# Mixed order of small expert units, weight splits on another engine, and an earlier pass over activations, in a fused Fourier-filter and mixture-of-experts kernel

## The chip, the cores and the metric

The kernel runs on one core of one Trainium2 chip. The metric is the device time of one execution in microseconds. A core has TensorE (PE; its weight loads are shown apart, as PEld), VectorE (DVE), ScalarE (ACT), GpSimd (POOL) and SyncE (SP), which issues most of the DMAs; GpSimd issues the DMAs that gather and scatter rows by index.

## The reference, cut to what matters

```python
def _attn_ref(x, filt_r, filt_i):            # x: 8 x 2496 x 256
    X = np.fft.rfft(x, axis=1)
    Y = X * (filt_r + 1j * filt_i)[None, :, :]
    return np.fft.irfft(Y, n=x.shape[1], axis=1).astype(np.float32)

def _moe_ref(x, w_gate, w_noise, noise, w1, w2):   # x: 19968 x 256, 8 experts, F = 1024
    noisy = x @ w_gate + np.log1p(np.exp(x @ w_noise)) * noise
    top2 = np.argpartition(-noisy, 2, axis=1)[:, :2]
    ...                                            # softmax over the two: top2_w
    for e in range(E):
        for k in range(2):
            mask = top2[:, k] == e
            h = np.maximum(x[mask] @ w1[e], 0.0)
            out[mask] += top2_w[mask, k, None] * (h @ w2[e])
```

The eight sequences ("batches") are filtered by a Fourier transform along the sequence, and every row of the result goes through two of eight experts.

## The kernel before, in words

Two streams of work share the engines. **The Fourier stream** (fft_stream) transforms one batch after the other with matrix products, writes the filtered rows to a DRAM tensor `y`, computes the gates, and appends each row's number to its expert's list in DRAM (`lst`). **The expert stream** (expert, fed by parts) takes up to 512 rows of one expert's list at a time, a block: GpSimd gathers the rows (gather), SyncE's DMA transposes them (flip), VectorE copies them apart (turn), TensorE multiplies by w1 (tiles `hps`), ScalarE and VectorE take the ReLU and split it in a high and a low half (`hh`, `hl`), TensorE multiplies by w2 (`yps`), ScalarE scales by the gate (`stage<-yps,gt`), and GpSimd adds the rows to `out` with an indirect DMA, the scatter. A scatter waits until the scatters of the unit ahead of it have landed; those of one unit do not wait for each other.

Every product is three products of halves (_mm3: high with high, high with low, low with high). **Until five batches are through (`ready < HALF`), the halves are float32r**: 21 weight loads of blocks, in each of which wsplit makes four high halves of w1 (`w1h`, ScalarE) and four low halves (`w1l`, 128x512), and the same for w2. From then on the halves are float16 with a power-of-two scale per expert and batch, which needs the largest weight and activation. These come from wscales, a generator that the Fourier stream moves on one step in every fourth of its own (write): 64 loads of weight tiles with a sum of squares each on ScalarE, powers (a short chain over VectorE and TensorE) for w1 and for w2, and 12 loads of rows of `y` of the first two batches, each with a maximum on VectorE (`ymax<-wp`); later batches take their maxima when their rows are written. gather for the first float16 block runs all steps that are then left, one behind the other, until `self.scaled` is set. xscale reduces the maxima to a scale.

**At the end** of the kernel the lists' remainders are done in units: 14 of 256 rows and 4 of 128, each of one expert. A unit loads its two float16 weight planes of 1 MB (load_planes) into one of three sets of buffers (`fr`, `fi`, `wb`), whatever its row count. Gathered rows lie in four slots of 128 rows in `stage`, taken in rotation (slot).

The instruction order on each engine is that of a list scheduler at build time, with parts pinned as written (pin); each engine then runs its list in order.

Of the kernel before, what the change touches and what calls it, by code (L numbers as in the profile page):

```python
# [22 lines left out]
NB, S, D = 8, 2496, 256  # L23
# [26 lines left out]
NUNIT = (LEFT + E * (UNIT // 2 - 1)) // UNIT  # L50
USUAL = LEFT // UNIT
ENDS = (UNIT, USUAL, NUNIT), (UNIT // 2, E // 2, E)
SW = 32
YW = D + E
LR = 128
# [73 lines left out]
def f32v(ap):  # L129
    return ap.bitcast(F32)  # L130
# [20 lines left out]
class Moe:  # L151
# [427 lines left out]
    def xscale(self, bt):  # L579

        nc = self.nc
        nc.vector.tensor_reduce(self.xm, self.ymax[:, :2 * bt + 2], axis=AX.XY, op=ALU.max)
        q = yield from self.powers(self.xm, 1, TX)
        t = self.xs[bt + 1] = self.cp.tile([128, 2], F32, name=f"xs{bt}")
        nc.vector.tensor_copy(t, q[:, :, 0])
        yield

    def wscales(self):


        nc, io, v = self.nc, self.io, self.nc.vector
# [11 lines left out]
        Y = [(bt, h, g) for bt in range(FIRSTS) for h in range(2) for g in range(0, NG, 8)]  # L603
# [27 lines left out]
        def pairs(first, then, n):  # L631
            old = []
            for i in range(n + 3):
                if i >= 3:
                    self.pin(then, *old.pop(0), hold=False)
                if i < n:
                    old.append((i, self.pin(first, i, hold=False)))
                yield

        yield from pairs(load, top, 8 * E)  # L640
        for a, t in enumerate((TW1, TW2)):
            q = yield from self.powers(self.wmax[:, a * E:a * E + E], E, t, True)
# [3 lines left out]
            else:  # L646
                v.tensor_mul(self.wtab[:, 2], self.wtab[:, 2], q[:, 1])
            yield
        yield from pairs(load_y, top_y, len(Y))
        self.scaled = True  # L650
        yield
        self.pin(load_all, 0)
# [483 lines left out]
    def gather(self, blk, i):  # L1136

        nc = self.nc
        lt, n, nt, s, tabi, ready = blk
        if i == 0:  # L1140
            self.ra = nc.gpsimd.value_load(tabi[0:1, 1, s:s + 1], min_val=0, max_val=E - 1)
            self.sc = None
            if ready >= HALF:
                while not self.scaled:
                    next(self.preps)
                self.sc = self.P.tile([128, 3, 1], F32, name="sc", bufs=3)
                nc.gpsimd.tensor_copy(self.sc, self.wtab[:, :, bass.ds(self.ra, 1)])
        w = None
        if self.tail(tabi):
            w = self.wodd = (self.wodd + 1) % 3  # L1150
            if nt < BLK // 128:
                w = self.load_planes(tabi, s, w)
        xg = []
        for t in range(nt):
            x = self.slot("xg")
            self.pin(lambda: nc.gpsimd.indirect_dma_start(  # L1156
                out=x.bitcast(I32), out_offset=None, in_=self.y[:BLK + ready * ROWS],
                in_offset=bass.IndirectOffsetOnAxis(ap=lt[:, i, t:t + 1], axis=0)),
                hold=False, only=[nc.gpsimd.engine])
            xg.append(x)  # L1160
        return xg, self.turns["xg"] + 1 - nt, self.ra, self.sc, w
# [138 lines left out]
    def wsplit(self, st, nm, sc):  # L1300
        nc, P = self.nc, self.P
        if len(st.shape) == 4:
            return st
        if nm == "w2":

            hl = P.tile([128, 2, 2, 256], R32, name="w2", bufs=4)
            h, l = hl[:, 0], hl[:, 1]
        else:
            h = P.tile([128, 2, 256], R32, name=nm + "h", bufs=4)
            l = P.tile([128, 2, 256], R32, name=nm + "l", bufs=4)  # L1310
        sv = st.rearrange("p (k f) -> p k f", k=2)
        if sc is not None:
            if nm == "w1":
                return self.pair(h, l, sv, sc[:, 0])
            hl = hl.rearrange("p a b c -> p (a b c)").bitcast(F16)[:, :1024].rearrange("p (a b c) -> p a b c", a=2, b=2)
            h, l = hl[:, 0], hl[:, 1]
            nc.scalar.activation(h, sv, AF.Copy, scale=sc[:, 1])
            nc.vector.scalar_tensor_tensor(l, sv, sc[:, 1], h, op0=ALU.mult, op1=ALU.subtract)
            return hl
        nc.scalar.copy(h, sv)  # L1320
        nc.vector.tensor_sub(l, sv, f32v(h))
        return hl if nm == "w2" else (h, l)

    def fetch(self, may):
# [81 lines left out]
    def run(self):  # L1406
# [15 lines left out]
        def parts():  # L1422
# [5 lines left out]
            for i in range(NB):  # L1428
# [5 lines left out]
                it = (self.read_list(i, s, m * BLK) for s in range(a, b))  # L1434
# [8 lines left out]
            for s in range(SINGLE):  # L1443
                yield from cut(self.read_list(NB, s, BLK), NB)
            self.more = [self.nc.values_load(self.tabs[NB + 1 + i][0:1, 0, n:n + 1], min_val=0, max_val=E * CAPB * BLK // u)  # L1445
                         for i, (u, n, _) in enumerate(ENDS)]
            it = (self.read_list(NB + 1 + i, s, u) for i, (u, n, _) in enumerate(ENDS) for s in range(n))
            soon = [next(it)]
            while soon:
                soon += [b for b in (next(it, None),) if b]  # L1450
# [14 lines left out]
        for _ in self.expert(parts(), may, fill):  # L1465
# [4 lines left out]
            if state["ready"] >= NB - 1:  # L1470
                state["k"] += 1
                if state["k"] % EVERY == 0:
                    next(self.preps, None)
        with self.tc.If(self.more[0] + self.more[1] < sum(E * CAPB * BLK // u for u, _, _ in ENDS)):
            self.sp = self.spw = None
            rest = (((*self.read_list(NB + 1 + i, s, u), NB), 0) for i, (u, a, b) in enumerate(ENDS) for s in range(a, b))
            for _ in self.expert(rest, lambda: True):
# [43 lines left out]
```

## Time and profile before

| | us |
|---|---|
| median of 3 runs | 2200.29 |
| lowest, highest | 2194.58, 2200.72 |
| the profiled execution's own time | 2191.23 |
| its span in the profile | 2189.4 |

The profile is one execution. Its rows are in microseconds from the start of the span. Lines are those of the kernel before (L1321 is the subtraction in wsplit, L1370 the low half of the ReLU, L1396 the gate's scaling, L1397 the scatter, L1156 the gather, L615 the maximum over rows of `y`, L599 the sum of squares).

### The profile page before, as it was taken

How to read it: one execution, taken by the hardware profiler on the slowest of the kernel's cores; microseconds unless marked ns; L12 is line 12 of the kernel's file. 1: busy time of each engine (PE TensorE's matmuls, PEld its weight loads, DVE VectorE, ACT ScalarE, POOL GpSimd, SP SyncE). 2: the span in 40 equal slices, each digit the busy share in tenths (PEclk: the TensorE clock that was granted, in tenths of full speed). 3: DMA queues.
4: the chain of work that ended last, by engine and by line, in shares of the span. 5: the costliest groups of instructions: out<-in, count | busy, mean ns of one | idle time of the engine just before them, and what ended most of it. 6: DMA issues, size and time to landing. Idle time of an engine off the chain costs nothing. (4 is left out here: it accounts for less than half of the span.)

```text
span 2189.4 us, 42880 instructions
## 1 busy us (share of the span) xinstructions
PE 2107.5 (96%) x14517; PEld 1596.5 (73%) x14517; DVE 1473.3 (67%) x3245; ACT 1286.4 (59%) x2505; POOL 1024.6 (47%) x946
## 2 busy tenths in 40 slices
PE   8779999999999999899999999999999999999996
PEld 6437888888888888666666666766666666667886
DVE  4866678767986787778766886579666664333443
ACT  6666774777567746665665556555566564333443
POOL 4133424533443343545544453544566555654653
PEclk9989999999999999999999999999999999999999
DMA  9688987999888866967766666856899999768996
GB/s 241 173 247 203 230 222 171 222 234 228 203 213 230 189 144 152 202 160 174 156 155 151 136 146 149 198 118 131 198 246 238 230 238 211 200 148 221 277 273 170
DMA packets 511675, 428.49 MB, mean 196 GB/s; under 512 B 215680, under 2 KB 397016, under 8 KB 511448
## 3 DMA queue, kind: packets, MB, share of 16 engines
q1 hardware_dynamic: 450135, 341.27, 59.2%
q0 software_dynamic: 61312, 84.40, 22.5%
q8 instruction: 116, 1.90, 0.4%
q14 instruction: 112, 0.91, 0.1%
HBM read 263.92 MB, written 122.03 MB: 176 GB/s over the span
## 5 line engine op out<-in xcount | busy, mean ns | idle before, releaser
L1397 POOL DMA_INDIRECT out<-stage,ids x316 | 527.3, 1669 | 339.8 <-ACT stage L1396 245.9
L1370 DVE SCALAR_TENSOR_TENSOR hl<-hps,hh 128x512 f16<-128x512 f32 (+3 forms) x712 | 432.2, 624 | 339.5 <-ACT hh L1369 279.1
L1156 POOL DMA_INDIRECT stage<-y,ids x316 | 348.4, 1103 | 538.2 <-DMA xt<-stage 425.5
L124 PE MATMUL yps<-w,hh 128*128 128x256 f16 (+1 forms) x2048 | 558.8, 279 | 9.0 <-ACT hh L1369 3.8
L125 PE MATMUL yps<-w,hh 128*128 128x256 f16 (+1 forms) x2048 | 553.2, 277 | 0.0
L126 PE MATMUL yps<-w,hl 128*128 128x256 f16 (+1 forms) x2048 | 543.4, 278 | 6.8 <-DVE hl L1370 6.5
L1369 ACT ACTIVATE hh<-hps 128x512 f16<-128x512 f32 (+3 forms) x712 | 375.6, 550 | 185.7 <-PE hps L126 161.6
L125 PE MATMUL hps<-mxl,w1h 128*128 128x512 f16 (+1 forms) x1024 | 394.3, 386 | 0.7 <-DVE mxl L1244 0.7
L126 PE MATMUL hps<-mxh,w1l 128*128 128x512 f16 (+1 forms) x1024 | 393.0, 385 | 0.0
L124 PE MATMUL hps<-mxh,w1h 128*128 128x512 f16 (+1 forms) x1024 | 385.5, 388 | 2.7 <-DVE hl L1370 1.7
L1396 ACT ACTIVATE stage<-yps,gt 128x256 f32<-128x256 f32 x316 | 143.2, 475 | 342.3 <-PE yps L126 169.8
L124 PEld LDWEIGHTS <-hh 128*128 128x128 f16 x1760 | 172.3, 98 | 51.3 <-ACT hh L1369 4.1
L126 PEld LDWEIGHTS <-hl 128*128 128x128 f16 x1760 | 171.5, 98 | 48.9 <-issue 3.0
L125 PEld LDWEIGHTS <-hh 128*128 128x128 f16 x1760 | 172.2, 98 | 38.1 <-issue 6.0
L126 PEld LDWEIGHTS yps<-w,hl 128*128 128x128 f32 x768 | 145.9, 192 | 15.8 <-DVE hl L1370 8.2
L124 PEld LDWEIGHTS yps<-w,hh 128*128 128x128 f32 x768 | 147.0, 192 | 12.5 <-ACT hh L1369 4.9
L125 PEld LDWEIGHTS yps<-w,hh 128*128 128x128 f32 x768 | 146.6, 192 | 4.4 <-issue 0.6
L542 ACT COPY yt<-q 117x1024 uint16<-117x1024 uint16 x96 | 90.8, 946 | 42.4 <-PE q L536 23.6
L126 PEld LDWEIGHTS <-w1l 128*128 128x128 f16 x640 | 62.6, 98 | 71.8 <-issue 1.1
L1226 DVE COPY stage<-xt 128x1024 uint16<-128x1024 uint16 (+2 forms) x174 | 109.8, 685 | 3.0 <-issue 1.9
L125 PEld LDWEIGHTS <-w1h 128*128 128x128 f16 x640 | 62.6, 98 | 54.0 <-issue 4.0
L124 PEld LDWEIGHTS <-w1h 128*128 128x128 f16 x640 | 62.6, 98 | 53.0 <-issue 6.2
(287 smaller groups left out, 4041.7 us busy)
## 6 DMA issues: line engine op xcount, KB each, us to landing
stage<-w SPq DMA_DIRECT2D x328, 256.0 KB
x<-x SPq DMA_DIRECT2D x88, 256.0 KB
fd<-c SPq DMA_DIRECT2D x77, 240.0 KB
fi<-wpl SPq DMA_DIRECT2D x18, 1024.0 KB
fx<-fd SPq DMA_DIRECT2D x140, 128.0 KB
out<-z SPq DMA_DIRECT2D x24, 702.0 KB
wp<-w SPq DMA_DIRECT2D x64, 256.0 KB
fr<-w SPq DMA_DIRECT2D x16, 1024.0 KB
```

The source lines that it names most:

```text
L124: nc.tensor.matmul(o, lh, rh, start=start, stop=False)
L125: nc.tensor.matmul(o, lh, rl, start=False, stop=False)
L126: nc.tensor.matmul(o, ll, rh, start=False, stop=stop)
L542: e = nc.scalar.copy(yt.bitcast(U16)[:, :k, :256].rearrange("p g (two d) -> p g two d", two=2), p.bitcast(U16)[:RP, :2 * m].rearrange("p ( ...
L1156: self.pin(lambda: nc.gpsimd.indirect_dma_start(out=x.bitcast(I32), out_offset=None, in_=self.y[:BLK + ready * ROWS], in_offset=bass.Indir ...
L1226: nc.vector.tensor_copy(xu.rearrange("p (t two) -> p two t", two=2), ent[3][0][:, 2 * kc:2 * kc + 2, :w])
L1369: hold(lambda: nc.scalar.activation(h, p, AF.Relu))
L1370: v = hold(lambda: nc.vector.scalar_tensor_tensor(l, p, 0.0, hf[0], op0=ALU.max, op1=ALU.subtract))
L1396: nc.scalar.activation(o, p, AF.Copy, scale=gate[:, t])
L1397: a = nc.gpsimd.indirect_dma_start(out=self.io["out"][:BLK + ready * ROWS], out_offset=bass.IndirectOffsetOnAxis(ap=ids[:, t:t + 1], axis= ...
```

## The change

There are four edits. parts takes the small units in an order written in MIXED: after every third unit of 256 rows or so stands one of 128, the last of them at the end. gather skips slots so that a unit's rows begin at a multiple of its own row count. wsplit subtracts on GpSimd in place of VectorE for w1 as long as the halves are float32r. wscales runs its 12 loads and maxima over `y` first, then the 64 sums over the weights; a flag `seen` marks that the maxima are done, and xscale asserts it.

```diff
+MIXED = sorted(((i, s) for i, (_, n, _) in enumerate(ENDS) for s in range(n)), key=lambda u: u[1] * 3 + 4 if u[0] else u[1])
...
     def xscale(self, bt):
 
         nc = self.nc
+        assert self.seen
...
+        yield from pairs(load_y, top_y, len(Y))
+        self.seen = True
         yield from pairs(load, top, 8 * E)
         for a, t in enumerate((TW1, TW2)):
             q = yield from self.powers(self.wmax[:, a * E:a * E + E], E, t, True)
...
-        yield from pairs(load_y, top_y, len(Y))
         self.scaled = True
...
+        while (self.turns.get("xg", -1) + 1) % nt:
+            self.slot("xg")
         xg = []
...
-        nc.vector.tensor_sub(l, sv, f32v(h))
+        (nc.gpsimd if nm == 'w1' else nc.vector).tensor_sub(l, sv, f32v(h))
...
-            it = (self.read_list(NB + 1 + i, s, u) for i, (u, n, _) in enumerate(ENDS) for s in range(n))
+            it = (self.read_list(NB + 1 + i, s, ENDS[i][0]) for i, s in MIXED)
```

Three places show what moves on the engines. Between them, from about the 31st block of the expert stream to the units, the orders are the same on every engine, and they are the same up to the first blocks.

GpSimd, one block of the float32r part, before: `gt` is the gate copy for the next block, `stage<-y` the gathers for the one after, `out<-stage` the scatters of an earlier block.

```order
L1178 COPY gt<-stage 128x4
L1156 DMA stage<-y,ids 128x264 x4
L1106 CAST ids<-lt 128x4
L1397 DMA out<-stage,ids 5660x256 x4
L1178 ISA
```

The same place in the change:

```order
L1183 COPY gt<-stage 128x4
L1326 TENSOR_TENSOR w1l<-stage,w1h 128x512 x3
L1161 DMA stage<-y,ids 128x264 x2
L1326 TENSOR_TENSOR w1l<-stage,w1h 128x512
L1161 DMA stage<-y,ids 128x264 x2
L1109 CAST ids<-lt 128x4
L1402 DMA out<-stage,ids 5660x256 x4
L1183 ISA
```

Three of a block's four subtractions stand between the gate copy and the first gather, the fourth behind two gathers.

VectorE, before, where the float32r part ends (the 23rd and 24th block): `ymax<-wp` are the maxima over rows of `y`, `hl` is the low half that TensorE's second product needs.

```order
L1370 SCALAR_TENSOR_TENSOR hl<-hps,hh 128x512 x2
L547 TENSOR_REDUCE ymax<-yt 117x1
L582 TENSOR_REDUCE xm<-ymax 128x1
L615 TENSOR_REDUCE ymax<-wp 117x1 x2
L1202 SCALAR_TENSOR_TENSOR w1l<-stage,sc,w1h 128x512
L1370 SCALAR_TENSOR_TENSOR hl<-hps,hh 128x512
L398 TENSOR_TENSOR tl<-fx,th 128x512
L615 TENSOR_REDUCE ymax<-wp 117x1
L1370 SCALAR_TENSOR_TENSOR hl<-hps,hh 128x512
```

The same place in the change, with the last two reductions over the weights' sums (`wmax`):

```order
L548 TENSOR_REDUCE ymax<-yt 117x1
L584 TENSOR_REDUCE xm<-ymax 128x1
L603 TENSOR_REDUCE wmax<-wquart 128x1
L399 TENSOR_TENSOR tl<-fx,th 128x512
L562 TENSOR_REDUCE pm<-xm 1x1
```

and the first of the 12 maxima in the change, at the second block of the expert stream:

```order
L1082 TENSOR_TENSOR ro<-ro,rx 56x128
L1249 TENSOR_TENSOR mxl_2204<-xps,mxh_2203 128x512
L617 TENSOR_REDUCE ymax<-wp 117x1
L1375 SCALAR_TENSOR_TENSOR hl<-hps,hh 128x512
L341 TENSOR_TENSOR xl<-x,xh 117x512
```

The 12 maxima left the end of the float32r part and stand within the second to fourth block of the stream. The 64 sums of squares on ScalarE all stood ahead of the 20th block, 13 of them ahead of the fourth; now none stands ahead of the fourth, and the last 11 stand between the 20th and the 23rd.

GpSimd, the end of the program, before: gate copies of one column are those of the 128-row units.

```order
L1397 DMA out<-stage,ids 21104x256 x2
L1178 ISA
L1178 COPY gt<-stage 128x1
L1180 TENSOR_SCALAR gt<-gt,sc,xs_20026 128x1
L1397 DMA out<-stage,ids 21104x256
L1178 ISA
L1178 COPY gt<-stage 128x1
L1180 TENSOR_SCALAR gt<-gt,sc,xs_20026 128x1
L1397 DMA out<-stage,ids 21104x256 x3
```

The same place in the change:

```order
L1402 DMA out<-stage,ids 21104x256 x2
L1183 ISA
L1183 COPY gt<-stage 128x1
L1185 TENSOR_SCALAR gt<-gt,sc,xs_20026 128x1
L1402 DMA out<-stage,ids 21104x256 x5
```

Before, the last four scatters are of four units of one scatter each. In the change the last five are two, two and one: two units of 256 rows and one of 128.

## Rows read from the trace of the kernel before

**Rows 1.** Windows: PE, PEld, DVE, ACT, POOL busy; TensorE clock; DMA share; GB/s.

```profile
200.00:850.00 650.00, 634.38 (x4090) 554.57 (x4089) 504.18 (x1105) 440.67 (x891) 267.41 (x217) 0.99 0.86 205
850.00:900.00 50.00, 42.99 (x279) 36.04 (x278) 36.10 (x63) 27.77 (x54) 24.33 (x23) 0.97 0.95 191
900.00:2000.00 1100.00, 1091.55 (x7596) 742.38 (x7595) 727.62 (x1474) 613.53 (x1121) 575.02 (x531) 1.00 0.78 181
2000.00:2150.00 150.00, 149.95 (x1381) 133.67 (x1380) 65.18 (x170) 65.66 (x171) 86.51 (x107) 1.00 1.05 260
2150.00:2174.00 24.00, 22.79 (x286) 20.27 (x283) 11.26 (x43) 10.86 (x40) 8.67 (x10) 1.00 0.72 211
```

**Rows 2.** Timeline of GpSimd, a scatter at 2122 and the last three.

```profile
2122.46 1.54 POOL L1397 DMA_INDIRECT out<-stage,ids  x1 [0.30 <-issue]
...
2169.94 1.59 POOL L1397 DMA_INDIRECT out<-stage,ids  x1 [6.30 <-ACT hh L1369]
2175.61 1.56 POOL L1397 DMA_INDIRECT out<-stage,ids  x1 [4.08 <-ACTq L1474]
2180.16 1.56 POOL L1397 DMA_INDIRECT out<-stage,ids  x1 [2.99 <-DMA out<-stage,ids]
```

**Rows 3.** Timeline of ScalarE: the gate's scaling ahead of these scatters.

```profile
2121.45 0.47 ACT L1396 ACTIVATE stage<-yps,gt 128x256 f32<-128x256 f32 x1 [1.75 <-PE yps L126]
...
2168.68 0.47 ACT L1396 ACTIVATE stage<-yps,gt 128x256 f32<-128x256 f32 x1 [0.85 <-issue]
...
2174.12 0.47 ACT L1396 ACTIVATE stage<-yps,gt 128x256 f32<-128x256 f32 x1 [0.86 <-PE yps L126]
```

**Rows 4.** The chain that ended last, in order of time: one piece.

```profile
2175.61 3.80 DMA out<-stage,ids
```

**Rows 5.** DMA issues of the page: a weight plane of the units.

```profile
fi<-wpl SPq DMA_DIRECT2D x18, 1024.0 KB
```

**Rows 6.** Window of 50 us in the units, columns as in rows 1.

```profile
2050.00:2100.00 50.00, 50.00 (x459) 44.49 (x458) 22.64 (x59) 22.41 (x58) 31.42 (x40) 1.00 1.07 281
```

**Rows 7.** Waits of TensorE from 869 to 896: us in total, times, longest.

```profile
PE yps L126 <- DVE hl L1370: 4.2, 2, 3.4
PE q L446 <- DVE a L428: 1.3, 1, 1.3
```

**Rows 8.** Groups on VectorE from 869 to 892: busy, mean ns, idle before.

```profile
L615 DVE TENSOR_REDUCE ymax<-wp 117x1 f32<-117x1024 bf16 (+1 forms) x9 | 10.0, 1125 | 4.1 <-DMA wp<-y 3.8 <-issue 0.3
```

**Rows 9.** Window of 5 us behind that wait, columns as in rows 1.

```profile
880.00:885.00 5.00, 3.35 (x15) 3.05 (x16) 4.75 (x7) 2.62 (x5) 3.92 (x4) 0.66 1.28 172
```

**Rows 10.** Single lines: duration ns min/median/max, first and last start.

```profile
L615 DVE TENSOR_REDUCE ymax<-wp x12: 929/1204/1221, 839.2 to 890.0; 117x1 f32<-117x1024 bf16 x8, 117x1 f32<-117x768 bf16 x4
L599 ACT ACTIVATE wp<-wp x64: 621/632/708, 187.4 to 734.8; 128x512 f32<-128x512 f32 x64
```

**Rows 11.** Groups by form: the subtraction on VectorE, a subtraction of that size on GpSimd.

```profile
L1321 DVE TENSOR_TENSOR w1l<-stage,w1h 128x512 fp32r<-128x512 f32 x84 | 57.7, 694 | 9.1 <-ACT w1h L1320 7.0 <-PE q L510 1.4 <-issue 0.6
L433 POOL TENSOR_TENSOR ab<-ab 128x512 f32<-128x512 f32 x10 | 12.7, 1271 | 9.5 <-DVE ab L432 9.5
```

**Rows 12.** Timeline of GpSimd in the float32r part: gate copy, first gather.

```profile
522.45 0.78 POOL L1178 COPY gt<-stage 128x4 f32 x1
530.91 1.02 POOL L1156 DMA_INDIRECT stage<-y,ids  x1 [7.68 <-DMA xt<-stage]
```

**Rows 13.** Timeline of VectorE in the same stretch: low halves of weights and rows.

```profile
533.29 0.69 DVE L1321 TENSOR_TENSOR w1l<-stage,w1h 128x512 fp32r<-128x512 f32 x1
534.49 0.68 DVE L1244 TENSOR_TENSOR mxl<-stage,mxh 128x512 fp32r<-128x512 f32 x1
```

**Rows 14.** Timeline at 70: VectorE beside a GpSimd subtraction, and alone.

```profile
69.73 1.35 DVE L894 TENSOR_TENSOR oh<-gz,m 117x176 f32<-117x176 f32 x1
...
72.98 0.34 DVE L894 TENSOR_TENSOR oh<-gz,m 117x176 f32<-117x176 f32 x1
...
69.62 1.26 POOL L428 TENSOR_TENSOR ab<-ab 128x512 f32<-128x512 f32 x1 [19.33 <-ACT yt L542]
```

## The prediction

> **What bounds the kernel now.** Read first the windows by stage [rows 1]. TensorE is busy for nearly every microsecond: it idles 15.6 us from 200 to 850 (650 less 634.38), 7.0 from 850 to 900, 8.5 from 900 to 2000, nothing from 2000 to 2150, 1.2 from 2150 to 2174, and then 15 us pass to the end of the span without a product. Since the change adds and removes no product, it can win only such idle time, or make more of it. The instruction order differs in two stretches: the first thirty blocks (to about 1000 us) and the units (from about 2000). So three places count: the last 15 us, the 7.0 us around 875, and the float32r part, in which the new work of GpSimd and VectorE must find cover.
>
> **The end: small units among large ones.** The last row of the chain that ended last is a scatter's DMA of 3.80 us, from its start to the landing [rows 4], and behind it the last scatter starts at 2180.16 [rows 2]. Its data was ready long before: ScalarE's last scaling ended at 2174.12 + 0.47 = 2174.59 [rows 3]. Where nothing holds a scatter, it starts soon after its scaling: 2121.45 + 0.47 = 2121.92 on ScalarE [rows 3], 2122.46 on GpSimd [rows 2], 0.54 us. So the last one could start at 2175.13 and starts 5.0 us later. It waits because each 128-row unit is one scatter that must wait for the landing of the one before; the last three start at 2169.94, 2175.61 and 2180.16 [rows 2], each held, while the scalings behind them are 2174.12 - 2168.68 = 5.44 us apart [rows 3]. In the new order a unit of 256 rows stands ahead of the last unit of 128. Its second tile is scaled by about 2169.15, its scatter starts at 2169.7 and lands 3.80 us later at 2173.5, before 2175.13. The wait is gone: -5.0 us. TensorE's 1.2 us of idle time among the four small units [rows 1] should partly go, since a small unit's chain then lies beside a large unit's products: -0.5, between -1.2 and 0.
>
> What this costs is DMA. A unit loads two planes of 1024 KB [rows 5], 2.10 MB, whatever its rows. A unit of 256 rows is 48 products of 256 columns and 48 of 256, 24576 columns, 10.24 us at 2.4 GHz, the level that a granted clock of 1.00 is [rows 1]. At 260 GB/s [rows 1] it moves 2.66 MB, so 0.56 MB beside the planes. Three large units and a small one want 4 x 2.10 + 3.5 x 0.56 = 10.36 MB in 3 x 10.24 + 5.44 = 36.2 us, 286 GB/s. The highest window shows 281 [rows 6], with TensorE at 50.00 of 50; by that the group takes 36.9 us, 0.7 more. If 260 were the ceiling, it would take 39.8, and three groups would lose 11 us, less what the buffers cover: a load is issued two units ahead, at least 10.24 + 5.44 = 15.7 us, and 2.10 MB at 260 GB/s take 8.1, so 7.6 are covered and about 3.5 stay. I take nothing, because the rate that is wanted is nearly one that was seen with no idle time; bound +3.5. Skipped slots cost no work; a gather may come half a unit later, which the two units of lead hide.
> The end: **-5.5 us**, bounds -6.2 and -1.5.
>
> **The float32r part's end: the maxima leave.** From 869 to 896 TensorE waits 4.2 us for VectorE's `hl` and 1.3 for its `a` [rows 7]. VectorE is late there because nine of the twelve maxima over `y` stand in that stretch: 10.0 us of work and 4.1 of waiting, most of it for their loads [rows 8], 14.1 of 23 us. After the longer wait the granted clock is 0.66 for 5 us with 3.35 of work [rows 9], a third of which is lost, about 1 us. Without the maxima: -6.5 us; at worst the wait is passed to something else, 0.
> In their place come the last 11 sums of squares, at 0.632 us [rows 10] 7.0 us on ScalarE, which is busy 27.77 of 50 there [rows 1], and they wait for loads too. If ScalarE's lateness reached TensorE as VectorE's did (5.5 us for 14.1), it would cost 5.5 x 7.0 / 14.1 = 2.7. I take +1.5, about the middle, as ScalarE has more room.
>
> **The float32r part's start: the maxima come.** Twelve maxima of 1.2 us [rows 10] are 14.4 us on VectorE in the first four blocks, with their loads. At the old rate, 5.5 us for nine, they would cost 7.3; but the subtractions of four blocks, 16 x 0.694 = 11.1 us [rows 11], leave VectorE there, and 13 sums leave ScalarE, 8.2 us. I take +2.5, bounds 0 and 7.3.
>
> **The subtraction on GpSimd.** 84 subtractions of 128x512 leave VectorE, 57.7 us, and cost 1.271 us each on GpSimd by the nearest row, 107 us [rows 11]. GpSimd has the time: 267 of 650 us are busy from 200 to 850 [rows 1]. What counts is where it sits in the queue. Behind the gate copy at 522.45 to 523.2 GpSimd waits 7.68 us for a transposition [rows 12]; the three subtractions that stand there in the new order take 3.8. The fourth stands behind two gathers of about a microsecond and starts near 534 or 535, where VectorE did it at 533.29, just before the rows' last low half at 534.49 [rows 13]; it is needed only in the last quarter of the products by w1, some 8 us on. Loads of w2 into the same slots wait for it on SyncE's queue, and transpositions stand behind them: a few tenths of a microsecond late per block. No gain either, since VectorE is not what TensorE waits for in most of this part. I take +1, bounds -2 (VectorE's relief) and +14 (see below).
> VectorE pays in another way. Beside a GpSimd subtraction that started at 69.62 and took 1.26, a small operation of VectorE took 1.35, and the same operation 0.34 when alone [rows 14]: it stood still until GpSimd was done. So the relief of 57.7 us shrinks by up to 84 x 1.01 = 85 us.
> The Trainium skill's page "SBUF — State Buffer", section "Who interferes with whom", speaks against this edit with just that: a VectorE instruction with two SBUF inputs and a GpSimd instruction that reads SBUF share a port, and the later one blocks wholly until the earlier ends. The trace agrees, by 1.01 us at the row named; by the page in full this edit's term would be the port's case among the rivals, by my reading of the rows it is the +1 above.
>
> **Sum.** -5.5 - 6.5 + 1.5 + 2.5 + 1 = -7.0 us. The profiled execution's 2191.23 would become 2184.2. It lies 9 us below the median of the runs, 2200.29, from which the forecast is **2193 us**.
>
> **Rivals.**
> *Only the end pays.* The generator's work is only traded between places: what the maxima cost at 875 they cost again at the start, and the sums the rest. For it: VectorE is as busy over 200 to 850 (504 of 650) as around 875 (36 of 50), and DMA is busy too (0.86) [rows 1]. Against: the subtractions leave. Time 2200.3 - 5.5 = 2195, within 0.3%.
> *The shared port decides.* If every subtraction holds VectorE for 1.01 us, VectorE gains 85 - 57.7 = 27 us of load; if half of that reaches TensorE, +13.5, in place of my +1. Against: the operation that was held reads both inputs from SBUF, while `hl`, which TensorE waits for, reads one from PSUM, and no row shows such a one held. 2193 + 12.5 = 2206; if only a quarter reaches it, 2199.
> *The subtraction is late: slower than before.* GpSimd's queue is in order, and a block's products by w1 cannot go on without `w1l`. If the late transposition or a held scatter keeps GpSimd from the subtractions, each of 21 weight loads stalls TensorE. It decides once 21 stalls eat the other terms and 0.3% more: (8.0 + 6.6) / 21 = 0.7 us each. At 1 us each: 2200.3 - 8 + 21 = 2213. For it: scatters stand ahead of the subtractions. Against: the 7.68 us of idle time [rows 12].
> *Planes come late among the units.* +3.5 and the idle gain lost: 2197.
>
> **Chances.** 0.3% of the time, 6.6 us, is about what a measurement of this kernel can tell from no change, and 2193 lies just beyond it. My forecast or better has 0.50, of which 0.05 would still read as the same; only the end 0.22 (0.02 faster, the rest the same); the port 0.11 (0.08 the same, 0.03 slower); the late subtraction 0.10, slower; the planes 0.07, the same. Faster 0.47, same 0.40, slower 0.13. The likeliest case alone runs from 2187 to 2197. For 8 in 10 I take 2185 to 2207: from every term at its good bound (-6.2 - 6.5 + 0 + 0 - 2, 2186, and a microsecond for the runs) to the port's case.
>
> **What would show it.** In the changed profile the last scatter starts within a microsecond of ScalarE's last scaling, and no two single scatters follow each other. No wait for `hl` over 2 us stands around 875. `w1l` takes about 1.3 us on GpSimd, lies in the gap behind the gate copy, and TensorE waits for GpSimd less than 3 us in all; some of VectorE's two-input operations take a microsecond more. In the units TensorE stays at full busy time. I am wrong if TensorE waits for GpSimd's `w1l` or VectorE's `hl` block after block, if the maxima make waits of several us near 200, or if a unit's first product waits for its plane.

## The result and the profile after

The changed kernel takes 2222.62 us (median of 6 runs, 2219.69 to 2228.79), the kernel before 2195.41 beside it (2190.59 to 2200.72): ratio 1.0127, 95% interval 1.0104 to 1.0149. It is 27 us slower where 2193 us, 0.3% faster, was forecast, and it lies outside the range. Its profiled span is 2220.1 us against 2189.4.

The windows by stage, columns as in [rows 1], the last one shifted to the changed kernel's end:

```profile
200.00:850.00 650.00, 611.97 (x3885) 526.49 (x3884) 503.52 (x987) 423.09 (x858) 349.57 (x286) 0.99 0.85 202
850.00:900.00 50.00, 47.74 (x310) 40.94 (x309) 30.11 (x79) 27.93 (x60) 20.36 (x22) 1.00 0.68 159
900.00:2000.00 1100.00, 1089.44 (x7556) 745.63 (x7556) 729.16 (x1477) 616.54 (x1128) 566.60 (x522) 1.00 0.78 176
2000.00:2150.00 150.00, 147.66 (x1312) 122.81 (x1311) 62.21 (x159) 61.62 (x159) 78.45 (x98) 1.00 0.96 254
2150.00:2210.00 60.00, 58.23 (x566) 50.51 (x565) 25.19 (x72) 26.49 (x73) 30.10 (x33) 1.00 0.84 222
```

Against [rows 1] TensorE idles 38.0 us from 200 to 850 instead of 15.6, and 2.3 us from 2000 to 2150 instead of none; from 850 to 900 it is busy 4.75 us more. VectorE, which was to be relieved by 57.7 us, is as busy as before from 200 to 850: 503.5 against 504.2.

Windows of time hide that the two kernels are at different work at one time. So count the products of the expert blocks (`hps`, `yps`; 11856 in both) and take each one's start, from the two traces:

| start of product | before | after | later by |
|---|---|---|---|
| 1536 | 501.4 | 515.9 | 14.6 |
| 3840 | 978.6 | 1002.9 | 24.3 |
| 8704 | 1782.2 | 1814.5 | 32.3 |
| the last | 2173.8 | 2210.1 | 36.3 |
| end of the span | 2189.4 | 2220.1 | 30.7 |

Of the 36.3 us, 24.3 are lost by product 3840, in the early, float32r stretch. Another 8.0 lie between products 3840 and 8704, where the instruction orders are the same. These can't be put down to the change: products 4224 to 8704 stand in one order in all twenty kernels whose traces are used here, and take 735.1 to 748.2 us in them (739.5 before, 748.2 after; the ten that take 735 are those of the sets of runs below in which the kernel before took 2178 to 2179 us). Among the units 4 us more go, and behind the last product 5.6 us come back, the gain that the end was to bring. That gain can be read on ScalarE and GpSimd. The first fence is ScalarE's last scaling, the second GpSimd's last two scatters (answering to [rows 3] and [rows 2]):

```profile
2210.41 0.47 ACT L1401 ACTIVATE stage<-yps,gt 128x256 f32<-128x256 f32 x1 [0.86 <-PE yps L127]
```

```profile
2206.82 1.56 POOL L1402 DMA_INDIRECT out<-stage,ids  x1 [0.62 <-ACT stage L1401]
2211.70 1.56 POOL L1402 DMA_INDIRECT out<-stage,ids  x1 [3.33 <-DMA out<-stage,ids]
```

2210.88 to 2211.70 is 0.8 us, where it was 5.6.

In the early stretch TensorE waits nowhere for GpSimd's subtraction by name. These are TensorE's largest waits from 200 to 850 (total, times, longest):

```profile
PE yps L127 <- DVE hl L1375: 8.9, 7, 2.5
PE yps L125 <- ACT hh L1374: 6.2, 5, 2.5
PE hps L125 <- DVE hl L1375: 4.3, 7, 1.4
PE yps L125 <- ACT stage L1401: 3.2, 2, 1.7
PE q L447 <- DVE a L429: 2.9, 2, 2.1
```

Many short waits, for VectorE and ScalarE. The subtraction itself, on GpSimd (group by form; answers to [rows 11]), and the waits of SyncE's queue for it from 150 to 980:

```profile
L1326 POOL TENSOR_TENSOR w1l<-stage,w1h 128x512 fp32r<-128x512 f32 x84 | 117.7, 1433 | 99.1 <-ACT w1h L1325 93.0 <-DMA stage<-w 5.4 <-DMA fd<-c 0.3
```

```profile
SPq L1287 <- POOL w1l L1326: 55.0, 39, 6.1
```

The subtraction takes 1.43 us on average, and SyncE's queue stands 55.0 us in all behind it.

### The profile page after: what moved, and what is told of

It reads as the page before. It is cut to its first block, busy times and chain, and to the rows that moved or that the text cites. A ratio compares the mean times of both kernels' runs of the same rounds, so it can differ in the third digit from the quotient of the medians.

```text
span 2220.1 us, 42897 instructions
## 1 busy us (share of the span) xinstructions
PE 2121.4 (96%) x14517; PEld 1595.5 (72%) x14517; DVE 1486.2 (67%) x3161; ACT 1283.1 (58%) x2505; POOL 1116.8 (50%) x1030
## 4 chain that ended last, share of the span: by engine, by line
PE 59%; DVE 3%; issue 1%; DMA 1%; ACT 1%; POOL 0%; POOLq 0%; DVEq 0%; SPq 0%; ACTq 0%
PE yps L127 9%; PE hps L127 9%; PE yps L125 9%; PE hps L125 9%; PE yps L126 9%; PE hps L126 9%; PE q L447 1%; DMA wp<-w 1%; DVE hl L1375 1%; PE q L511 1%; PE u L458 0%; PE q L535 0%; ACT hh L1374 0%; PE q L536 0%; PE q L537 0%
## 5 line engine op out<-in xcount | busy, mean ns | idle before, releaser
L1161 POOL DMA_INDIRECT stage<-y,ids x316 | 340.3, 1077 | 472.6 <-DMA xt<-stage 365.4
L1326 POOL TENSOR_TENSOR w1l<-stage,w1h 128x512 fp32r<-128x512 f32 x84 | 117.7, 1433 | 99.1 <-ACT w1h L1325 93.0
L1231 DVE COPY stage<-xt 128x1024 uint16<-128x1024 uint16 (+2 forms) x174 | 128.1, 788 | 0.0
L126 PEld LDWEIGHTS <-w1h 128*128 128x128 f16 x640 | 62.7, 98 | 58.3 <-issue 9.1
```

What stands on the lines that cost most here:

```text
L126: nc.tensor.matmul(o, lh, rl, start=False, stop=False)
L1161: self.pin(lambda: nc.gpsimd.indirect_dma_start(out=x.bitcast(I32), out_offset=None, in_=self.y[:BLK + ready * ROWS], in_offset=bass.Indir ...
L1231: nc.vector.tensor_copy(xu.rearrange("p (t two) -> p two t", two=2), ent[3][0][:, 2 * kc:2 * kc + 2, :w])
L1326: (nc.gpsimd if nm == 'w1' else nc.vector).tensor_sub(l, sv, f32v(h))
```

## The experiments

Each is timed beside the kernel before on the same chip. From one set of runs to the next that kernel's median lay between 2178.1 and 2195.3 us (on one and the same chip at 2190.9 and 2178.1), so ratios to it are compared, not times.

### Each edit alone

**The changed kernel without the subtraction's edit, the subtraction alone, the maxima alone, the units alone.** The first and second edit one line:

```diff
-        (nc.gpsimd if nm == 'w1' else nc.vector).tensor_sub(l, sv, f32v(h))
+        nc.vector.tensor_sub(l, sv, f32v(h))
```

(the second the other way round, in the kernel before); the third moves `yield from pairs(load_y, top_y, len(Y))` ahead of the weights' `pairs`; the fourth has MIXED and the slots' alignment alone.

> The changed kernel with the first-layer float32r subtraction back on VectorE; the unit order and the maxima stay as changed. Theory (the subtraction costs the time): at equal counts of expert matmuls the changed kernel had lost 24 us by its 3840th, all inside the stretch in which GpSimd subtracts, so this kernel stands about 24 to 30 us under the changed one, 2193 to 2199 us, within 0.3% of the kernel before. Rival (the maxima ahead of the weights' sums, by moving VectorE's work into the first 250 us, cost the time): it stays near 2215 to 2223.

> The kernel before with the one line of the subtraction on GpSimd. Theory: the loss comes with this line alone, 20 to 30 us above the kernel before, 2215 to 2226 us. Rival (the maxima cost it): 2195 within 5 us.

> The kernel before with the y maxima ahead of the weights' sums. Theory (the subtraction costs the time): within 0.3% of the kernel before, and if the prediction's terms hold (6.5 us of waits near 870 leave, 1.5 and 2.5 come back) 2.5 us under it, 2193. Rival (the maxima cost the time): 15 to 27 us above it, 2210 to 2222.

> The kernel before with units of 128 rows among those of 256 and the slots' alignment alone. The prediction has 5.5 us under the kernel before, 2190. The rival from the changed kernel's trace: the end after the last matmul is 5.6 us shorter (10.0 against 15.6 us), but the matmuls' starts in the units stretch lose 4.0 us more in waits for the hand-offs, so that only about 1.5 us are left, 2194.

| kernel | us | ratio | 95% interval |
|---|---|---|---|
| changed, without the subtraction's edit | 2222.55 | 1.0140 | 1.0108 to 1.0172 |
| the subtraction alone | 2231.30 | 1.0187 | 1.0153 to 1.0220 |
| the maxima alone | 2221.04 | 1.0115 | 1.0085 to 1.0146 |
| the units alone | 2198.21 | 1.0019 | 0.9997 to 1.0040 |

The theory that the subtraction alone costs the time fell: without it nothing comes back. But the subtraction alone costs more (36 us) than all edits together (27), and so the costs do not add. Both edits share one thing: the scheduler, which orders by simulated times, makes a new order of all engines from the first blocks to about the 30th whenever one early instruction changes. The maxima's edit changes no instruction's engine, shape or number, only order. So order and engine had to be separated.

The units alone leave the early stretch alone (product 3840 starts 0.5 us later, 8704 at the same time). Their last product starts 10.3 us later and the end of the span comes 5.1 us later, so 5.2 us come back at the end, as forecast, and twice that is lost before. TensorE's waits from 1900 to 2190:

```profile
PE yps L125 <- ACT hh L1372: 4.2, 6, 0.9
PE hps L125 <- ACT mxh L1204: 0.4, 1, 0.4
PE hps L125 <- DMA fi<-wpl: 0.3, 1, 0.3
```

In the kernel before, from 1900 to 2180, the first of these is

```profile
PE yps L124 <- ACT hh L1369: 0.8, 3, 0.3
```

and two windows with the units alone (columns as in [rows 1]):

```profile
2050.00:2065.00 15.00, 13.40 (x138) 10.98 (x136) 5.62 (x18) 5.39 (x16) 10.42 (x13) 1.00 1.04 303
2065.00:2070.00 5.00, 4.53 (x24) 2.88 (x22) 1.17 (x4) 1.96 (x6) 1.79 (x6) 0.66 1.07 242
```

Five of the six waits for ScalarE's relu (`hh`) stand within 4 us of a seam, a change between large and small units; the likely reason, which is not tested, is that a small unit's products are too short to cover it. Behind 1.6 us of idle time the granted clock is 0.66 over 5 us, a mean of the levels of 2.4 and 1.2 GHz. The named waits make 4.9 of the 10.3 us, the lower clock in this window about 1.7 (0.34 of 5 us); the rest has no name in the trace. The planes are nearly innocent: one wait of 0.3 us in all, and none in the window that shows 303 GB/s.

**The four small units together, one large unit last.**

```diff
-MIXED = sorted(..., key=lambda u: u[1] * 3 + 4 if u[0] else u[1])
+MIXED = sorted(..., key=lambda u: USUAL - 1.5 if u[0] else u[1])
```

> The kernel before with the slots' alignment and another order of the units: thirteen of 256 rows, the four of 128, and the last of 256 behind them. Theory (a last unit of 256 rows saves 5.3 us behind the last matmul, 10.1 against 15.3 us, and the units of 128 that stand apart cost 10.4 us in hand-offs, as the waits before their matmuls show): with the four together only two changes of size remain, the hand-offs cost 1 to 3 us and 2 to 4 us stay, 2191 to 2194. Rival (any unit of 256 behind one of 128 waits for its planes): no gain, 2195 to 2199.

2192.58 us, 1.0005 (0.9986 to 1.0024). No gain that can be told, and none lost; a gain of 2 to 4 us is at the edge of this interval, so the two theories are not told apart by the time. The rival's mechanism does not show in the trace: no product among the units waits for a plane by name. The longest wait there, 3.5 us, is for VectorE's `hl` in the last small unit.

### The order held

Order-only dependencies (they wait for nothing but the place in the queue) between each instruction and the one ahead of it in a recorded order hold every engine to that order:

```diff
+def hold_order(tc, bb):
+    here, last = {i.name: i for i in bb.instructions}, {}
+    for n in names:                # the recorded order
+        i = here.get(f"I-{n}")
...
+            tc.add_manual_dep(i, p.name, mybir.DependencyInfo(
+                mybir.DependencyClass.NoSync, mybir.DependencyReason.DATA), reason="order as recorded")
```

**The subtraction on GpSimd in the order of the kernel before**, and **the order that the subtraction's edit makes, with the subtraction on VectorE.**

> The kernel before with the first-layer float32r subtraction on GpSimd, and every engine's order held to that of the kernel before by order-only dependencies, so that the 84 subtractions alone change their engine. Theory (the new order of the whole early stretch costs the 36 us of the same edit, not GpSimd): 2188 to 2202 us, within 0.3% of the kernel before. Rival (GpSimd's slower subtraction, its queue or the shared port costs it): 2215 to 2232.

> The other corner: all engines held to the order that the scheduler made for the subtraction on GpSimd, but the subtractions stay on VectorE, so that no instruction changes its engine against the kernel before. Theory (the order costs it): 2220 to 2235 us, as with the subtraction on GpSimd in that order (2231). Rival (the engine costs it): 2190 to 2202.

| order | subtraction on VectorE | on GpSimd |
|---|---|---|
| of the kernel before | 1 | 2210.44 us, 1.0085 (1.0059 to 1.0110) |
| made for GpSimd | 2212.97 us, 1.0099 (1.0076 to 1.0123) | 1.0187 (above) |

Neither theory is right alone: the engine costs 0.85%, the order 0.99%, and together they make the 1.87%. Some 19 us come from 84 instructions on another engine, and some 22 us from an order in which nothing changes its engine. (In the traces the order on every engine is indeed the recorded one, but for a few neighbours that start together.)

What the engine does can be seen here with nothing else moved. Groups by form from 150 to 1000 on VectorE, before and then with the subtraction on GpSimd:

```profile
L1226 DVE COPY stage<-xt 128x1024 uint16<-128x1024 uint16 x54 | 37.4, 746 | 2.7 <-issue 1.9 <-DMA xt<-stage 0.8
L1244 DVE TENSOR_TENSOR mxl<-stage,mxh 128x512 fp32r<-128x512 f32 x44 | 30.0, 682 | 1.2 <-ACT mxh L1243 0.8 <-issue 0.2
```

```profile
L1226 DVE COPY stage<-xt 128x1024 uint16<-128x1024 uint16 x52 | 47.3, 963 | 1.8 <-issue 1.6 <-DMA xt<-stage 0.2
L1244 DVE TENSOR_TENSOR mxl<-stage,mxh 128x512 fp32r<-128x512 f32 x44 | 43.6, 991 | 2.0 <-ACT mxh L1243 1.7 <-issue 0.2
```

The rows' low halves `mxl`, which stand next to the weights' in every block, rise from 682 to 991 ns, 1821 for the 12 that overlap a subtraction. The extreme, VectorE first, then GpSimd:

```profile
394.88 4.79 DVE L1244 TENSOR_TENSOR mxl<-stage,mxh 128x512 fp32r<-128x512 f32 x1
```

```profile
394.78 4.33 POOL L1321 TENSOR_TENSOR w1l<-stage,w1h 128x512 fp32r<-128x512 f32 x3
```

One VectorE instruction of 0.68 us stands through three subtractions in a row and ends behind the last. Over 150 to 1040, 169 VectorE instructions overlap a subtraction and take 45.4 us more than their own medians in the kernel before; 57.7 us of relief shrink to 12. `hl`, which reads PSUM, is not lengthened: 44 of the 169 are `hl`, at a mean of 683 ns, and its longest of the 216 from 150 to 1000 is 694 ns.

TensorE feels it. Its waits for VectorE from 150 to 980 make 11.0 us in the kernel before and 20.3 us here; those for ScalarE rise from 16.7 to 21.0, those for GpSimd from nothing to 1.5. (Both are sums over the rows of the view of TensorE's waits.) The window, columns as in [rows 1], and two of those rows, before:

```profile
150.00:980.00 830.00, 803.49 (x5153) 679.25 (x5154) 634.31 (x1397) 553.97 (x1099) 333.54 (x281) 0.99 0.85 201
PE yps L126 <- DVE hl L1370: 6.2, 5, 3.4
PE hps L125 <- DVE mxl L1244: 0.7, 2, 0.4
```

and with the subtraction on GpSimd, with two rows that are new:

```profile
150.00:980.00 830.00, 789.33 (x5019) 670.77 (x5020) 616.01 (x1281) 541.44 (x1075) 425.05 (x353) 0.98 0.84 196
PE yps L126 <- DVE hl L1370: 3.6, 2, 2.7
PE hps L125 <- DVE mxl L1244: 3.5, 3, 1.7
PE yps L126 <- DVE w1l L1202: 3.6, 1, 3.6
PE q L534 <- DVE tl L521: 3.3, 1, 3.3
```

The same can be asked of every pair of kernels here that have one order and differ in the subtraction's engine: the order of the kernel before as it is, with late squares and with small loads (both below), the order made for GpSimd, and the changed kernel's order as it is and with late squares. In all six pairs TensorE's waits for VectorE grow with the subtraction on GpSimd, by 5 to 13 us; its waits for ScalarE change by -1.5 to +4.3 us and those for GpSimd by at most 2.9. Each trace is a single execution, but the six agree. And SyncE's queue waits for `w1l`, before and now:

```profile
SPq L1282 <- DVE w1l L1321: 22.9, 17, 7.4
```

```profile
SPq L1282 <- POOL w1l L1321: 53.0, 35, 9.4
```

These waits do not make the queue slower as a whole: all its waits from 150 to 980 are 375.5 us before and 359.3 us here. The queue waits longer for `w1l` and less for other things.

**Lateness without GpSimd**: the subtraction on VectorE, later in VectorE's held order, and **the subtraction on GpSimd in four pieces**, in the held order of the kernel before:

```diff
-        (nc.gpsimd if nm == 'w1' else nc.vector).tensor_sub(l, sv, f32v(h))
+        if nm == 'w1':
+            for k in range(2):
+                for o in (0, 128):
+                    nc.gpsimd.tensor_sub(l[:, k, o:o + 128], sv[:, k, o:o + 128], f32v(h)[:, k, o:o + 128])
+        else:
+            nc.vector.tensor_sub(l, sv, f32v(h))
```

> The order of the kernel before held, the subtraction on GpSimd in four pieces of 128x128 instead of one of 128x512 (in one piece: 1.0085 of the kernel before). Theory (VectorE's instructions beside the subtraction stand until it ends, 45 us in all): they can go in between pieces, the 45 us fall to under 25 and the ratio to 1.002 to 1.006. Rival (the planes' low parts are late by GpSimd's own time): four instructions take longer than one of 1.3 us, and the ratio is 1.0085 to 1.013.

> The order of the kernel before held, the subtraction on VectorE, but 71 of its 84 instructions 1 to 4 VectorE instructions later, so that the planes' low parts come later without GpSimd. On GpSimd their mean time behind the high part rose from 1.73 to 2.64 us and the ratio to 1.0085. Theory (VectorE's instructions that stand beside GpSimd's are what costs, not the lateness): ratio 0.998 to 1.003. Rival (the lateness costs it): 1.005 to 1.010.

In pieces: 2204.50 us, 1.0106 (1.0085 to 1.0128), by the rival. But it does not decide: the time that VectorE loses beside them fell only from 45.4 to 39.3 us, while the four pieces of a plane take 2.2 us (172.6 / 80, the first fence, a group by form) instead of 1.4, and the queue's wait rose to 74.0:

```profile
L1324 POOL TENSOR_TENSOR w1l<-stage,w1h 128x128 fp32r<-128x128 f32 x320 | 172.6, 627 | 60.2 <-ACT w1h L1320 37.2 <-DVE oc L1059 18.9 <-ACT th L520 2.4
```

```profile
SPq L1282 <- POOL w1l L1324: 74.0, 49, 6.1
```

Late on VectorE: 2192.99 us, 1.0063 (1.0041 to 1.0085), the rival's too. The low half's mean distance behind the high half (end to end, over 84) is 1.73 us before, 2.64 on GpSimd and 3.10 here; the queue's wait:

```profile
SPq L1282 <- DVE w1l L1321: 63.5, 31, 11.8
```

So lateness alone costs: 1.37 us for each of 84 instructions is 0.63%, though TensorE's waits for `w1l` stay at 0.2 us in all. The way from there to TensorE is not shown. The load of the next weights into the freed slot waits for the subtraction, and on SyncE's queue everything stands behind that load; but a longer wait of that queue is not by itself a loss. All its waits are 398.6 us here, 375.5 in the kernel before, and 401.5 in the kernel with small loads below, which is the fastest of all.

If the cost is in proportion, GpSimd's 0.91 us make 0.42% of its 0.85% (an estimate from these two runs), and the other half is left for what VectorE stands beside GpSimd. The pieces do not fit that split well: their low halves end 2.11 us later than in the kernel before (3.84 us behind the high half), which by the same proportion is 0.97% of their 1.06%, though VectorE still loses 39.3 us beside them. So lateness is at work for certain, VectorE's standing beside GpSimd probably, and how the 0.85% divides between them stays open. What speaks for VectorE's part is TensorE's waits: late on VectorE, the subtraction raises those for VectorE by 3.2 us and those for ScalarE by 6.0; on GpSimd it is 9.3 and 4.3.

### Where an order loses

**Late squares.** On ScalarE the squares of the weights' sums stand so early that they wait for their 256 KB load, and ScalarE with them. Their group from 150 to 1000, in the kernel before, with the maxima alone, and in the order made for GpSimd with the subtraction on VectorE:

```profile
L599 ACT ACTIVATE wp<-wp 128x512 f32<-128x512 f32 x64 | 40.9, 640 | 53.6 <-DMA wp<-w 45.7 <-issue 7.0 <-DVE wmax L601 0.6
```

```profile
L600 ACT ACTIVATE wp<-wp 128x512 f32<-128x512 f32 x64 | 40.7, 635 | 62.7 <-DMA wp<-w 61.2 <-DVE rx L1080 1.1 <-DVE wmax L602 0.2
```

```profile
L599 ACT ACTIVATE wp<-wp 128x512 f32<-128x512 f32 x64 | 40.6, 635 | 70.5 <-DMA wp<-w 69.2 <-issue 1.2
```

So the squares were moved behind up to 4 of ScalarE's next instructions (where needed VectorE's reductions over the sums move with them), the rest of the order held: in the kernel before, with the maxima alone, with the subtraction on GpSimd, and in the other order. Only the recorded list of the order differs from the kernel that each starts from.

> The kernel before, its order held except that 48 of the 64 squares of the weights' sums on ScalarE stand 4 ScalarE instructions later, and 9 others up to 3 later (7 can't move). In the kernel before 33 squares wait in ScalarE's queue for their 256 KB load, 45.9 us in all, 50.1 to 70 us in the slower orders. Theory (ScalarE's waits for these loads are what an order gains or loses by): those waits fall under 15 us and the time by 5 to 15 us, to 2180 to 2190. Rival (they lie beside other work): 2193 to 2200, no change.

> The kernel with the maxima's edit alone (2221 us), its order held except that 48 of the 64 squares on ScalarE stand 4 of its instructions later. ScalarE waits 61.3 us there for the squares' loads, 45.9 us in the kernel before. Theory (this edit's loss comes through these waits): 2200 to 2212 us. Rival (as in the kernel before, where the same step took 31.7 us of such waits away and the time stood still): 2216 to 2226.

> Subtraction on GpSimd in the order of the kernel before (2210 us), with the squares 4 ScalarE instructions later. Theory (late weight loads hold SP's queue, behind it a square's load comes late, and ScalarE stands 5 to 6 us at 514 and 715 us): 2193 to 2202. Rival (GpSimd's instruction stretches VectorE's beside it, 45 us in all, and that costs the time): 2206 to 2214.

> The order that the scheduler made for the subtraction on GpSimd, the subtraction on VectorE (1.0099 of the kernel before), with the squares on ScalarE up to 4 instructions later. ScalarE waits 69.2 us for the squares' loads in that order. Theory (this order loses by the squares' waits, as the maxima's edit did): 1.002 to 1.006. Rival (it loses in other places): 1.008 to 1.012.

| order | waits for the loads, us | ratio without | with late squares |
|---|---|---|---|
| of the kernel before | 45.7 to 14.2 | 1 | 1.0009 (0.9993 to 1.0026) |
| the maxima alone | 61.2 to 27.0 | 1.0115 | 1.0039 (1.0022 to 1.0056) |
| before, subtraction on GpSimd | 57.6 to 21.3 | 1.0085 | 1.0084 (1.0060 to 1.0109) |
| made for GpSimd, on VectorE | 69.2 to 16.8 | 1.0099 | 1.0051 (1.0031 to 1.0070) |

Two new orders get back two thirds and a half of their loss. The old order, where as much waiting was taken away, gains nothing, and GpSimd's part is not touched. The waits are thus one channel of a new order's loss, and not worth their length: where the order is the old one, TensorE's work covers them.

**Small loads.** In the kernel before, and with the subtraction on GpSimd, orders held:

```diff
-            nc.sync.dma_start(t, io["w1" if i < 4 * E else "w2"][i // 4 % E, i % 4])
+            nc.sync.dma_start(t[:, :16], io["w1" if i < 4 * E else "w2"][i // 4 % E, i % 4, :, :16])
...
-            nc.scalar.activation(t, t, AF.Square, accum_out=self.wquart[:, i % 4:i % 4 + 1])
+            nc.scalar.activation(t[:, 16:].rearrange("p (a b) -> p a b", b=16), t[:, :16].unsqueeze(1).to_broadcast([128, 31, 16]),
+                                 AF.Square, accum_out=self.wquart[:, i % 4:i % 4 + 1])
```

> The kernel before, its order held, with the 64 loads for the weights' sums cut from 256 KB to 8 KB: 16 of 512 columns are loaded, and the square sums those 16 columns 31 times; so the weights' scales come from a part of them. It takes 15.9 MB from the queue of the early stretch. Theory (these loads are on the path in the early stretch): 10 to 25 us under the kernel before, 2168 to 2184. Rival (they lie beside TensorE's work): 2188 to 2196.

> The same small loads (16 of 512 columns in the weights' sums), with the subtraction on GpSimd, in the same order. Theory (GpSimd's cost of 19.5 us passes through the loads of the sums): within 6 us of the kernel with small loads alone. Rival (VectorE's instructions beside GpSimd's are what costs): 12 to 20 us above it.

2166.63 us, 0.9944 (0.9921 to 0.9966), and 2182.79, 1.0016 (1.0001 to 1.0031). What the loads bring beyond 8 KB each is worth 12 us of the kernel before, all of them. Whether that is because ScalarE waits less for them or because other loads get through sooner, this run does not tell. GpSimd's cost stays: 0.72% between the two, 16 us, within the rival's range, so it does not pass through the size of these loads. That VectorE's instructions are what costs, the rival's reason, does not follow from the time alone.

### Repairs on the changed kernel

Its order held; the squares late; the subtraction back on VectorE; both.

> The changed kernel (1.0127 of the kernel before), its order held, with 56 of the 64 squares on ScalarE 1 to 4 instructions later. Theory (two causes that add: VectorE beside GpSimd's subtractions, and squares that wait for their loads): the second part goes, 8 to 17 us, ratio 1.005 to 1.009. Rival (the subtraction alone sets it): 1.011 to 1.014.

> The changed kernel with its order held and the subtraction back on VectorE, so that 84 instructions alone change their engine. Theory (two causes): 10 to 20 us go, ratio 1.004 to 1.008. Rival (the order alone costs it): 1.010 to 1.014.

> Both at once on the changed kernel: subtraction back on VectorE, 57 squares later, else the changed kernel's order. Theory (two causes that add): little of the 27 us is left, ratio 0.998 to 1.003. Rival (other losses of the new order, such as its maxima at the start and its units): 1.005 to 1.010.

Late squares: 2211.42 us, 1.0144 (1.0120 to 1.0168). Back on VectorE: 2198.55, 1.0077 (1.0055 to 1.0100). Both: 2196.32, 1.0076 (1.0053 to 1.0099). Of the changed kernel's 1.27% about 0.5 are the engine's (0.7 with the squares late: 1.0144 against 1.0076); in the other orders it is 0.72 to 0.88. Late squares give nothing here, though ScalarE's waits for those loads fell from 53.2 to 19.7 us and from 62.0 to 25.7: the theory of two causes that add fell in its second part. Some 0.76% stay with this order. The units' share of it is about 0.2% by the run of that edit alone, whose interval reaches 1; where the rest sits is not settled.

No version tried computes everything and beats the kernel before.

## Why the prediction was wrong

**The end, -5.5: the mechanism was right, the sum was not.** The last scatter starts 0.8 us behind its scaling (0.5 with the units alone), and about 5 us came back, as worked out. But "TensorE's 1.2 us of idle time among the four small units should partly go" is the wrong way round: with the units alone the last product starts 10.3 us later, 4.9 us of it in waits, most of them at the seams between large and small units, and some in a fall of the clock. The edit measures about +4 us (-0.7 to +8.8) instead of -5.5. The planes' DMA, bounded at +3.5, makes one wait of 0.3 us.

**The maxima, -6.5 + 1.5 + 2.5: right where they left, wrong in the sum.** The stretch from 850 to 900 did become better by 4.75 us, with no wait for `hl` there. At the start VectorE does stand for their loads; the group of twelve has 8.4 us of such waits in the changed kernel, and with the maxima alone one is the longest:

```profile
268.09 0.95 DVE L616 TENSOR_REDUCE ymax<-wp 117x1 f32<-117x768 bf16 x1 [6.31 <-DMA wp<-y]
```

How much of these waits reached TensorE is not shown, so the +2.5 is neither borne out nor refuted. Yet the edit costs 25 us alone. The step that failed is "in their place come the last 11 sums of squares": it prices 11 sums, and all 64 stand elsewhere, each 103 to 219 us later with the maxima alone (the first at 304.3 us, before at 187.4). 17 of the 25 us come back when the squares are placed later on ScalarE, so most of the loss goes with ScalarE's waits for their loads in that order; the prediction took +1.5 for the sums.

**The subtraction, +1 (-2 to +14): mis-sized in both of its parts.** In an unchanged order it costs 18.6 us (0.85% of 2190.9), beyond its upper bound. "A few tenths of a microsecond late per block" was worked out from one block in which GpSimd had time; over 84 the mean is 0.91 us, and such lateness alone, on VectorE, was enough for 0.63% at 1.37. The price was looked for in TensorE's wait for `w1l`, of which there is next to none (1.5 us in that run, none in the changed kernel). SyncE's queue does wait for `w1l` as the prediction said ("Loads of w2 into the same slots wait for it"), 53.0 us instead of 22.9, but its waits as a whole do not grow. What grows is TensorE's wait for VectorE, from 11.0 to 20.3 us, and the sentence "VectorE is not what TensorE waits for in most of this part" kept that out of the sum. VectorE's stand beside GpSimd, 45 us, is 0.54 us for each subtraction, about half of the port rival's 1.01; that rival looked in the right place, though how much of the 18.6 us is VectorE's standing and how much the late subtraction stays open. The Trainium skill's page "SBUF — State Buffer", section "Who interferes with whom", has a VectorE instruction with two SBUF inputs and a GpSimd instruction that reads SBUF contend for one port pair, where the one that is later blocks wholly; by `mxl` the trace agrees (1821 against 682 ns). It counts copies in a two-port mode in as well; the 16-bit copy of `xt` was indeed held (1239 ns for the 23 that overlap, against 746), which the port rival had not counted. `hl`, with one input in PSUM, stayed free, as both have it.

**The sum: what was left out.** The prediction read that the instruction order differs in the first thirty blocks, and then priced only the instructions that the diff moves, in the order of the kernel before. The order that the subtraction's edit makes costs 22 us with every instruction on its old engine, and the changed kernel's own order costs 0.77%, 17 us, with the units' and the maxima's edits in it. That term was in no rival. It and the subtraction's term each break the range alone: 2193 - 1 + 18.6 is 2211, and 1.0077 x 2195.4 is 2212, both beyond 2207 (estimates from the runs above). It is also the likely reason why the parts do not add: the subtraction and the maxima alone, 1.87 and 1.15%, each contain a new order, and the changed kernel has only one.

## What to carry to other kernels

Where a scheduler that simulates times sets the order, an edit of one early instruction is an edit of all engines' orders, and the four orders made anew here cost 0.77 to 1.40% with the subtraction left on VectorE (two of them with the units' edit in it). Give the reordering a term of its own, or hold the order and change one thing. When work is moved to an idle engine, count two things that the move itself does not show: what it takes from the engine that it was to relieve (45 of 57.7 us here), and how much later its result comes (0.91 us each here), since lateness alone can cost where nobody waits for the result by name. A wait of a queue has a price only where it reaches the engine that bounds the kernel. A short unit put between long ones saves the tail once and can pay at every seam.

## What the runs showed of the hardware

In two places of the held run VectorE's two-input instruction stood through all subtractions that followed each other on GpSimd: `mxl` through three, 4.79 us in place of 0.68, and a subtraction `b` at 502.64 through two, 2.82 us. It is not always so: three of VectorE's copies of `xt` (at 462.94, 560.49 and 587.64) ended 0.4 to 0.7 us after the second of two subtractions had started, well ahead of its end, and that subtraction took 1.5 to 1.8 us where the median is 1.3. Cutting the subtraction in four freed VectorE little (45.4 to 39.3 us) and cost GpSimd 2.2 us a plane instead of 1.4. And 45.7 us of ScalarE's waits for 256 KB loads are without a loss that can be told in one order, while 17 us of loss went with 61.2 us of such waits in another.
